# Layer normalization moved from GpSimd to VectorE, and query weights, bias copies and weight loads placed elsewhere

## The chip, the cores and the metric

The kernel runs on one core of a Trainium2 chip. A core has engines[...]: TensorE (PE in the profile, its weight loads PEld), VectorE (DVE), ScalarE (ACT), GpSimd (POOL) and SyncE (SP), which here only issues transfers. The metric is the device time of one execution in microseconds (us), lower is better.

## The reference

Inputs q, k and v are [8, 8, 576, 64] (batch, head, token, head dimension) in float32. The first part is a linear attention with positive features, the second a gated MLP with a mixing over tokens:

```python
def phi(x):
    proj = einsum('bhsd,df->bhsf', x, w_phi)              # 64 -> 128
    proj = proj - max(abs(proj), axis=-1, keepdims=True)
    return concatenate([exp(proj), exp(-proj)], axis=-1)
kv  = einsum('bhsf,bhsd->bhfd', phi(k), v)
z   = sum(phi(k), axis=2)
x   = einsum('bhsf,bhfd->bhsd', phi(q), kv) / (einsum('bhsf,bhf->bhs', phi(q), z)[..., None] + 1e-6)
h   = maximum(x_as_[8, 576, 512] @ w_in, 0)               # 512 -> 1024
u, v = h[..., :512], h[..., 512:]
v_n = (v - mean(v)) / sqrt(var(v) + 1e-6)                 # over the 512 features
v_s = einsum('ts,bsd->btd', w_spatial, v_n) + b_spatial[None, :, None]
out = (u * v_s) @ w_out
```

## The kernel before, in words

Each batch has 576 tokens: 512 main tokens, held as four groups of 128 on the partitions, and 64 tail tokens. Two batches form a group and share the partitions for their tails. The work is cut into 36 units: for each batch four units of two heads (main tokens), and for each group one tail unit. In order they are batch 0 (units 0, 1, 3, 4, with the tail of group 0 as unit 2 between them), batch 1 (5 to 8), the tail of group 1 (9), batch 2 (10 to 13), batch 3 (14 to 17), the tail of group 2 (18), batches 4 and 5 (19 to 26), the tail of group 3 (27), batches 6 and 7 (28 to 35).

The order of work is written out by a loop over steps, one for each unit. A step calls the stages in a fixed order: keys, queries, attention, sums, next, features, out, maxima. Each stage works on the unit that its lag gives, so that several units are in flight. After every stage `fill` takes tasks of the gated MLP from a queue by a credit of TensorE time, and so puts their matmuls between those of the attention. When a batch's attention is done, its tasks are queued: the v half (matmul, relu on ACT, statistics on DVE), the root, the normalization, the u half, the spatial product, and the output product. `at(i, f)` puts a load or a small job after step i. A helper, `pin`, keeps such instructions in program order; the profile gives all of them the line L61.

What the stages put on the engines:

- keys: `ps` (L267) on PE; the row maxima `mk` on DVE (L279); the exponentials `kf` on ACT (L282); the factors `em` on ACT (L302); on POOL the scaled values `vs` (L307), or for a tail `vst`, by `tail_scale`, two multiplications and a copy for each of two batches.
- queries: maxima `mq` on DVE (L293), their split into a high and a low part `mhl` (L296, L297), on DVE for the first five units and on POOL after. The maxima stage transposes `mhl` on PE (L328, `pt`).
- features: the projected queries minus their maxima, exponentiated as `qf` on ACT (L366). For units of batches 2 and up ("merged") one matmul does projection and subtraction (L345), with weights `wm`, which hold `wphi` for one of two heads and rows of minus one from `sel` for the maxima. Copies `qT_b` and `qt` on DVE (L331, L332) put the maxima beside the queries.
- sums and attention: `pv` from `vs` and `kf` (L379, L381) and `pn` from `kv` and `qf` (L399), the quotient `x` on DVE (L389, L390).
- the MLP: `pv` (L448), `vr` on ACT (L450), statistics on DVE (L451, L452), root on POOL (L458 to L461), normalization `vn` and for tails `vnt` on POOL (L465), `pu` (L503), the spatial product `ps` (L524, L525), the gate `uT` on DVE (L527), the output `po` (L549) and its copy `ob` (L552).

The spatial weights are loaded as `wsp`, `wspr` and `wspt` and transposed on PE (L216, L218, L225, L226) into `w_spT`, during the first batch's tasks. Its two bias rows are copied on ACT after that (L230, L233). PSUM is used as eight banks. Loads that convert to bf16 (k, q and the weights) are issued by POOL, the v loads and transposing loads by SP.

Of the kernel before, what the change touches and what calls it, by code (L numbers as in the profile page):

```python
# [8 lines left out]
FP32 = mybir.dt.float32  # L9
BF16 = mybir.dt.bfloat16  # L10
AF = mybir.ActivationFunctionType
ALU = mybir.AluOpType
# [4 lines left out]
def kernel(  # L17
# [15 lines left out]
    nc = tc.nc  # L33

    B, H, S, D = q.shape
    F = w_phi.shape[1]
    DM = moe_w_in.shape[0]
    DFF = moe_w_in.shape[1]
    HALF = DFF // 2
    P = 128  # L40
    KC = DM // P
    NP = H // 2
    NB = 4
    T0 = NB * P
    TL = S - T0
# [4 lines left out]
    cpool = ctx.enter_context(tc.tile_pool(name="const", bufs=1))  # L50
# [3 lines left out]
    small = ctx.enter_context(tc.tile_pool(name="small", bufs=3))  # L54
    s2 = ctx.enter_context(tc.tile_pool(name="stage_b", bufs=2))
# [4 lines left out]
    def pin(start):  # L60
        return lambda *a, **kw: tc.keep_in_program_order(start(*a, **kw))  # L61
# [12 lines left out]
    XB = 2  # L74
# [14 lines left out]
    def half_tile(x, b, y):  # L89
        if b not in st:  # L90
            alloc(b)
        if st[b][x][y] is None:
            n = f"{x}_bf{(2 * b + y) % 4}"
            st[b][x][y] = ld.tile([P, 4, NB * D], BF16, tag=n, name=n, bufs=1)
        return st[b][x][y]
# [44 lines left out]
    ident = cpool.tile([P, P], BF16)  # L140
# [3 lines left out]
    wphi2 = cpool.tile([P, 2 * F], BF16)  # L144
    pin(nc.vector.memset)(wphi2, 0.0)
    neghalf = cpool.tile([P, NB + 1], FP32)
    pin(nc.vector.memset)(neghalf, -0.5)

    w_spT = cpool.tile([P, NB + 2, S], BF16)
# [4 lines left out]
    for i in range(NM):  # L154
        for tiles, name in ((mhl, "mhl"), (mT, "mT")):
            t = cpool.tile([P, P], BF16, name=f"{name}{i}")
# [4 lines left out]
    wm = cpool.tile([P, H, F], BF16)  # L161
    sel1 = cpool.tile([P, H], BF16)
    sel = cpool.tile([P, H, F], BF16)
    pin(nc.vector.tensor_tensor)(out=sel1, in0=ident[:, 0:H], in1=ident[:, H:2 * H], op=ALU.add)
    pin(nc.vector.tensor_scalar)(out=sel, in0=sel1.unsqueeze(2).to_broadcast([P, H, F]), scalar1=-1.0,
                                 scalar2=None, op0=ALU.mult)
    vst = [cpool.tile([P, 2, 2, H, DA], BF16, name=f"vst{i}") for i in range(2)]
    vnt = [cpool.tile([P, 2, HALF], BF16, name=f"vnt{i}") for i in range(2)]
# [4 lines left out]
    def fill_vnt(i, copy):  # L173
        for bl, row in ((0, TL), (1, 0)):
            pin(copy)(out=vnt[i][:, bl, :], in_=ident[:, row:row + 1].to_broadcast([P, HALF]))

    pin(nc.scalar.copy)(out=vst[0].rearrange("p b s h d -> p (b s h d)"), in_=zero.to_broadcast([P, 4 * H * DA]))
    for y in range(2):
        r = slice(y * D, (y + 1) * D)
        pin(nc.scalar.copy)(out=wphi2[r, y * F:(y + 1) * F], in_=wphi_f[r, :])  # L180
    for i in range(2):
        fill_vnt(i, nc.gpsimd.tensor_copy)
    for x in ("k", "q"):
        pin(nc.gpsimd.tensor_copy)(out=half_tile(x, 0, 0)[:, 2:4], in_=first[x, 2])
    load("k", 0, 1, 0, 2)
# [5 lines left out]

    w_in_bf = cpool.tile([P, KC, DFF], BF16)
    w_out_bf = cpool.tile([P, KC, DM], BF16)
    wsp = s2.tile([P, NB, T0], BF16, tag="vn", name="wsp", bufs=2)
    wspr = cpool.tile([P, NB, TL], BF16)
    wspt = s2.tile([TL, S], BF16, tag="ob", name="wspt", bufs=6)
    bsp_row = s2.tile([P, S], FP32, tag="xT", name="bsp_row", bufs=3)
    nc.sync.dma_start(out=bsp_row[TL:TL + 1, :], in_=moe_b_spatial)
# [2 lines left out]
    rows = moe_w_spatial[0:T0, :].rearrange("(p c) s -> p c s", c=NB)  # L201
    cols = moe_w_in.rearrange("(kc p) f -> p kc f", p=P)
# [7 lines left out]
    def transpose_spatial(i):  # L210

        pt = psum.tile([P, S], BF16, tag="bank", name="pt")
        if i < NB:
            sc = POS[i]
            for tp, c in enumerate(POS):
                nc.tensor.transpose(out=pt[:, tp * P:(tp + 1) * P], in_=wsp[:, c, bass.ds(sc, P, step=NB)],  # L216
                                    identity=ident)
            nc.tensor.transpose(out=pt[:, T0:S], in_=wspt[:, bass.ds(sc, P, step=NB)],  # L218
                                identity=ident[:TL, :TL])
            nc.vector.tensor_copy(out=w_spT[:, i, :], in_=pt)  # L220
            return
        for bl in range(2):
            lo = bl * TL
            for tp, c in enumerate(POS):
                nc.tensor.transpose(out=pt[lo:lo + TL, tp * P:(tp + 1) * P], in_=wspr[:, c, :], identity=ident)  # L225
            nc.tensor.transpose(out=pt[lo:lo + TL, T0:S], in_=wspt[:, T0:S], identity=ident[:TL, :TL])  # L226
            nc.vector.tensor_copy(out=w_spT[lo:lo + TL, NB + bl, :], in_=pt[lo:lo + TL, :])
        for bl, row in ((0, TL), (1, 0)):
            r = slice(row, row + 1)
            pin(nc.scalar.copy)(  # L230
                out=w_spT[r, NB + bl, 0:T0].rearrange("o (a b p) -> o a b p", a=2, b=2),
                in_=bsp_row[r, 0:T0].rearrange("o (p b a) -> o a b p", a=2, b=2))
            pin(nc.scalar.copy)(out=w_spT[r, NB + bl, T0:S], in_=bsp_row[r, T0:S])  # L233


    def merged(u):
        return u["pair"] and u["b"] >= XB

    def weights_with_max(n):
        for j in range(4 * n, 4 * n + 4, 2):  # L240
            pin(nc.gpsimd.tensor_copy)(out=wm[:, j, :], in_=wphi2[:, 0:F])
            pin(nc.gpsimd.tensor_tensor)(out=wm[:, j + 1, :], in0=wphi2[:, F:2 * F], in1=sel[:, j + 1, :], op=ALU.add)
            pin(nc.gpsimd.tensor_copy)(out=wm[D:D + 2 * H, j, :], in_=sel[0:2 * H, j, :])

    def q_even(u):
        u["qE"] = qts[u["i"] % len(qts)]
# [205 lines left out]
        nc.vector.bn_aggr(out=mv[r], in_=stats[r])  # L452

    def root(mv, r, n):

        var = small.tile([P, NB, 1], FP32, tag="var", name="var")
        rs = small.tile([P, NB, 2], FP32, tag="rs", name="rs")
        nc.gpsimd.tensor_scalar(out=var[r, 0:n], in0=mv[r, 0:n, 1:2], scalar1=1e-6, scalar2=None, op0=ALU.add)  # L458
        nc.gpsimd.tensor_tensor(out=rs[r, 0:n, 0:1], in0=var[r, 0:n], in1=neghalf[r, 0:n].unsqueeze(2), op=ALU.pow)
        nc.gpsimd.tensor_tensor(out=var[r, 0:n], in0=mv[r, 0:n, 0:1], in1=rs[r, 0:n, 0:1], op=ALU.mult)  # L460
        nc.gpsimd.tensor_scalar(out=rs[r, 0:n, 1:2], in0=var[r, 0:n], scalar1=-1.0, scalar2=None, op0=ALU.mult)  # L461
        return rs

    def normalize(dst, src, rs):
        nc.gpsimd.tensor_scalar(out=dst, in0=src, scalar1=rs[:, 0:1], scalar2=rs[:, 1:2],  # L465
                                op0=ALU.mult, op1=ALU.add)

    def b_v(b, j):
        d = st[b]
# [8 lines left out]
    def b_root(b):  # L478
        st[b]["rs"] = root(st[b]["mv"], slice(0, P), NB)

    def b_ln(b, j):
        d = st[b]
        normalize(d["vn"][:, j, :], d["vr"][j], d["rs"][:, j, :])

    def b_v_tail(g, bls):
        d = gs[g]
        r = slice(bls[0] * TL, (bls[-1] + 1) * TL)
        vr = s2.tile([P, HALF], BF16, tag="vr", name="vr", bufs=5)
        stats = small.tile([P, 6], FP32, tag="stats", name="stats")
        mv = small.tile([P, 1, 2], FP32, tag="mv_t", name="mv_t")  # L490
        v_mm(lambda kc: d["xTt"][:, kc, r], vr, r, stats, mv[:, 0, :])
        rstd = root(mv, r, 1)
        for bl in bls:
            r = slice(bl * TL, (bl + 1) * TL)
            normalize(vnt[g % 2][r, bl, :], vr[r], rstd[r, 0, :])

    def b_u(b, dc):
        d = st[b]
# [176 lines left out]
    AT, AB, XP = 5, 6, 3  # L675
    io = {}

    def at(i, f, *a):
        io.setdefault(i, []).append(lambda: f(*a))

    at(1, load_v, 1)
    at(2, load, "k", 1, 0)
    at(2, load, "q", 1, 0)
    at(3, load, "k", 1, 1)
    at(3, load, "q", 1, 1)
    at(4, load_weight, w_in_bf[:, :, HALF:DFF], cols[:, :, HALF:DFF])
    at(4, load_weight, wspt, moe_w_spatial[T0:S, :])
    at(5, tail_scale, 0, 1)
    at(5, load_weight, wsp, rows[:, :, 0:T0])
    at(5, load_weight, wspr, rows[:, :, T0:S])  # L690
    at(6, load_weight, w_in_bf[:, :, 0:HALF], cols[:, :, 0:HALF])
    at(8, load_weight, w_out_bf, moe_w_out.rearrange("(kc p) f -> p kc f", p=P))
    for u in units:
        i = u["i"]
        if not u["pair"] and u["g"] > 0:
            early = 1 if u["g"] > 1 else 0
            at(i - AT - early, load_tail, "k", u["g"])
            for x in ("q", "v"):
                at(i - AT + 1 - early, load_tail, x, u["g"])
        if u["pair"] and u["b"] >= XB:  # L700
            if u["pj"] == 0:
                for n, (x, y) in enumerate((("k", 0), ("q", 0), ("k", 1), ("q", 1))):
                    at((4, 4, 6, 7)[n] if u["b"] == XB else i - AB + n, load, x, u["b"], y)
                for y in range(2):
                    at(i - AB + 1 + 2 * y, load_v, u["b"], y)
            for x in ("k", "q"):
                at(i - XP, cross, x, u)
    at(6, weights_with_max, 0)
    at(7, weights_with_max, 1)
    for u in units:  # L710
        if merged(u):
            at(u["i"] - 1, q_even, u)
# [36 lines left out]
```

## Time and profile before

| what | value |
|---|---|
| time, median of 3 runs | 283.42 us (283.27 to 283.42) |
| span of the profiled execution | 282.7 us |
| mean granted TensorE clock | 0.986 |
| busy: PE, DVE, ACT, POOL | 257.1, 231.2, 219.5, 200.5 us |
| POOL: vs L307 (64), vn L465 (32 of 128x512) | 65.5, 24.3 us |
| DVE: mk L279 (72), mq L293 (62) | 47.7, 39.8 us |
| DVE: statistics L451 (40), gate L527 (32) | 26.7, 22.0 us |
| shares of the chain that ended last: PE, POOL, ACT, DVE, DMA | 62, 12, 9, 6, 4% |

The busy time counts only the execution of instructions, not waiting. The chain that ended last is followed back from the last instruction, at each step to what released it; an engine with a large share of it held up the end, wherever its busy share is small. A wait for several semaphores is put down to the one that came last. Over 40 slices of the span (7.07 us each), the busy tenths of PE and POOL and the clock are:

```profile
PE   2777979986999999999999999999999999999993
POOL 5988999999859886799949974889548832511710
PEclk9979999999799999999999999999999999999999
```

### The profile page before, as it was taken

What the parts mean: (1) busy time and instruction counts of PE and PEld (TensorE: products, weight loads), DVE (VectorE), ACT (ScalarE), POOL (GpSimd) and SP (SyncE); (2) the same over time, 40 slices, a digit from 0 to 9 for tenths busy, and PEclk for the clock granted to TensorE, in tenths of its full rate; (3) what the DMA queues carried; (4) which work ended last, traced back from release to release, by engine and by line L of the source; (5) the groups of instructions that cost most, each with busy time, mean ns of one, the idle gap of its engine ahead of it and who ended that gap; (6) DMA issues with size and microseconds to landing.
All of it is one profiled execution on the core that took longest, in us unless ns stands there. A gap on an engine that the chain in (4) does not pass through costs nothing.

```text
span 282.7 us, 8134 instructions
## 1 busy us (share of the span) xinstructions
PE 257.1 (91%) x3001; PEld 173.1 (61%) x3042; DVE 231.2 (82%) x576; ACT 219.5 (78%) x499; POOL 200.5 (71%) x362
## 2 busy tenths in 40 slices
PE   2777979986999999999999999999999999999993
PEld 1466866754776667666666775766666765654441
DVE  7979987875799979998889989998889897566341
ACT  5689996978399997899889987899699977723601
POOL 5988999999859886799949974889548832511710
PEclk9979999999799999999999999999999999999999
DMA  7989999999986999989989999999766301120305
GB/s 205 238 205 125 152 144 217 111 164 195 225 87 163 130 243 196 162 206 210 214 96 130 207 252 138 200 214 217 86 122 132 86 2 68 46 77 37 112 3 186
DMA packets 85148, 42.43 MB, mean 150 GB/s; under 512 B 52146, under 2 KB 80498, under 8 KB 85108
## 3 DMA queue, kind: packets, MB, share of 16 engines
q1 hardware_dynamic: 60020, 30.95, 55.0%
q0 software_dynamic: 24928, 10.89, 34.9%
q8 instruction: 24, 0.39, 0.6%
q14 instruction: 16, 0.13, 0.2%
q10 hardware_dynamic: 160, 0.07, 0.1%
HBM read 32.85 MB, written 9.44 MB: 150 GB/s over the span
## 4 chain that ended last, share of the span: by engine, by line
PE 62%; POOL 12%; ACT 9%; DVE 6%; DMA 4%; issue 4%; SPq 0%; POOLq 0%; ACTq 0%; DVEq 0%
PE ps L524 9%; PE pv L448 9%; PE po L549 9%; PE ps L267 6%; PE pu L503 6%; ACT kf L282 5%; PE pv L379 4%; PE pn L399 4%; PE pq L345 3%; DMA q_bf<-in_q_dram 3%; PE ps L525 2%; POOL vs L307 2%; POOL vst L61 2%; DVE stats L451 2%; ACT qf L366 2%
## 5 line engine op out<-in xcount | busy, mean ns | idle before, releaser
L282 ACT ACTIVATE kf<-ps 128x512 bf16<-128x512 f32 x144 | 76.2, 637 | 9.9 <-DVE mk L279 9.5
L307 POOL TENSOR_TENSOR vs<-v_f,em 128x512 bf16<-128x512 f32 x64 | 65.5, 1044 | 19.0 <-ACT em L302 17.6
L366 ACT ACTIVATE qf<-pq 128x512 bf16<-128x512 f32 x128 | 66.6, 620 | 9.6 <-PE pq L345 8.5
L279 DVE TENSOR_REDUCE mk<-ps 128x4 f32<-128x512 f32 x72 | 47.7, 677 | 1.2 <-PE ps L267 0.5
L293 DVE TENSOR_REDUCE mq<-ps 128x4 f32<-128x512 f32 x62 | 39.8, 680 | 2.6 <-PE ps L267 1.4
L524 PE MATMUL ps<-w_spT,vn 128*128 128x512 bf16 x116 | 33.1, 384 | 3.6 <-POOL vn L465 3.1
L527 DVE TENSOR_TENSOR uT<-ps,uT 128x512 bf16<-128x512 f32 x32 | 22.0, 687 | 16.8 <-PE ps L525 16.8
L451 DVE BATCH_NORM_STATS2 stats<-vr 128x6 f32<-128x512 bf16 (+1 forms) x40 | 26.7, 684 | 7.3 <-ACT vr L450 6.9
L549 PE MATMUL po<-w_out_bf,uT 128*128 128x512 bf16 x121 | 32.0, 380 | 0.4
L503 PE MATMUL pu<-xT,w_in_bf 128*128 128x512 bf16 x121 | 31.5, 380 | 0.5 <-issue 0.2
L448 PE MATMUL pv<-w_in_bf,xT 128*128 128x512 bf16 x116 | 30.7, 380 | 0.7
L450 ACT ACTIVATE vr<-pv 128x512 bf16<-128x512 f32 (+1 forms) x40 | 23.5, 615 | 7.6 <-PE pv L448 5.9
L379 PE MATMUL pv<-vs,kf 128*128 128x66 bf16 x512 | 24.3, 194 | 1.3 <-ACT kf L282 1.3
L390 DVE TENSOR_TENSOR x<-pn,rc 128x256 bf16<-128x256 f32 x64 | 24.9, 417 | 0.3
L465 POOL TENSOR_SCALAR vn<-vr,rs 128x512 bf16<-128x512 bf16 x32 | 24.3, 766 | 1.1
L399 PEld LDWEIGHTS <-qf 128*128 128x128 bf16 x512 | 20.5, 99 | 7.1 <-issue 1.4
L505 ACT ACTIVATE uT<-pu 128x512 bf16<-128x512 f32 x32 | 19.7, 641 | 4.9 <-PE pu L503 3.2
L379 PEld LDWEIGHTS <-kf 128*128 128x128 bf16 x512 | 21.8, 97 | 2.5 <-issue 1.5
L552 ACT COPY ob<-po 128x512 f32<-128x512 f32 x18 | 11.0, 614 | 14.9 <-PE po L549 8.4
L399 PE MATMUL pn<-kv,qf 128*128 128x66 bf16 x512 | 22.0, 195 | 0.3 <-ACT qf L366 0.3
L381 PE MATMUL pv<-vst,kf 128*128 128x66 bf16 x128 | 21.2, 192 | 0.0
L524 PEld LDWEIGHTS <-vn 128*128 128x128 bf16 x128 | 11.7, 98 | 13.8 <-POOL vn L465 4.6
(133 smaller groups left out, 572.2 us busy)
## 6 DMA issues: line engine op xcount, KB each, us to landing
out_dram<-ob SPq DMA_DIRECT2D x32, 256.0 KB, 2.5
v_f<-in_v_dram SPq DMA_DIRECT2D x14, 512.0 KB, 7.0
k_bf<-in_k_dram POOLq DMA_DIRECT2D x14, 256.0 KB, 6.3
q_bf<-in_q_dram POOLq DMA_DIRECT2D x14, 256.0 KB, 6.4
qt<-qT_b SPq DMA_DIRECT2D x24, 64.0 KB, 4.2
v_tl<-in_v_dram SPq DMA_DIRECT2D x8, 128.0 KB, 3.4
v_f<-in_v_dram SPq DMA_DIRECT2D x1, 1024.0 KB, 9.4
w_in_bf<-in_moe_w_in_dram POOLq DMA_DIRECT2D x2, 512.0 KB, 10.5
```

The lines of the kernel that those rows point to most:

```text
L279: nc.vector.tensor_reduce(out=u["mk"][:, hs], in_=pk, axis=AX.X, op=ALU.max, apply_absolute_value=True)
L282: nc.scalar.activation(out=u["kf"][:, s, hs, :], in_=pk, func=AF.Exp, bias=0.0, scale=sc)
L293: nc.vector.tensor_reduce(out=mq[:, 4 * half:4 * half + 4], in_=pq, axis=AX.X, op=ALU.max, apply_absolute_value=True)
L307: nc.gpsimd.tensor_tensor(out=vs[:, s, :, 0:D], in0=st[u["b"]]["v"][:, pj * H:(pj + 1) * H, :], in1=em[:, s, :].unsqueeze(2).to_broadcast( ...
L366: nc.scalar.activation(out=qf[:, s], in_=pq, func=AF.Exp, bias=0.0, scale=sc)
L379: nc.tensor.matmul(out=pv[:, hh, s, :], lhsT=u["kf"][:, s, 4 * hh + c, :], rhs=u["vs"][:, s, 4 * hh + c, :], start=(c == 0), stop=False)
L399: nc.tensor.matmul(out=pn[:, pos, :], lhsT=u["qf"][hh][:, s, pos, :], rhs=d["kv"][:, 2 * u["pj"] + hh, s, :], start=(s == 0), stop=(s == 1))
L448: nc.tensor.matmul(out=pv[r], lhsT=lhs(kc), rhs=w_in_bf[:, kc, HALF:DFF], start=(kc == 0), stop=(kc == KC - 1))
L451: nc.vector.bn_stats(out=stats[r], in_=dst[r])
L503: nc.tensor.matmul(out=pu, lhsT=w_in_bf[:, kc, dc * P:(dc + 1) * P], rhs=d["xT"][:, kc, :], start=(kc == 0), stop=(kc == KC - 1))
L524: nc.tensor.matmul(out=ps, lhsT=d["vn"][:, sp, cs], rhs=w_spT[:, sp, 0:T0], start=(sp == 0), stop=False)
L549: nc.tensor.matmul(out=po[r], lhsT=lhs(dc), rhs=w_out_bf[:, dc, :], start=(dc == 0), stop=(dc == KC - 1))
```

## The change

It has four parts. The normalization of v moves from POOL to DVE: it takes (v - mean) * rs directly from the statistics, so the root needs two operations, one on DVE (variance plus epsilon) and the power on POOL, where before it had four on POOL. The merged query weights `wm` are built by three wide instructions at the start (two on ACT, one on POOL), where before twelve narrow ones on POOL came after steps 6 and 7. The bias copies of ACT come after steps 1 and 2 instead of behind the transposition of the spatial weights. The loads of the spatial weights become one transfer fewer (`wsp` takes all 576 columns, `wspr` goes) and, with those of w_in, w_out, the group-1 tail and batch 2, are placed at other steps. It is meant to unload POOL and to bring each load and copy when it is needed. Lines of the changed file stand up to four higher or lower than those above.

```diff
--- before.py
+++ after.py
@@ -180,6 +180,14 @@
         pin(nc.scalar.copy)(out=wphi2[r, y * F:(y + 1) * F], in_=wphi_f[r, :])
     for i in range(2):
         fill_vnt(i, nc.gpsimd.tensor_copy)
+    def alternate(t, i):
+        return t.rearrange("p (j two) f -> p j two f", two=2)[:, :, i, :]
+    pin(nc.scalar.copy)(out=alternate(wm, 0), in_=wphi2[:, 0:F].unsqueeze(1).to_broadcast([P, NP, F]))
+    pin(nc.scalar.copy)(out=alternate(wm[D:D + 2 * H], 0), in_=alternate(sel[0:2 * H], 0))
+    pin(nc.gpsimd.tensor_tensor)(out=alternate(wm, 1), in0=alternate(sel, 1),
+                                 in1=wphi2[:, F:2 * F].unsqueeze(1).to_broadcast([P, NP, F]), op=ALU.add)
     for x in ("k", "q"):
         pin(nc.gpsimd.tensor_copy)(out=half_tile(x, 0, 0)[:, 2:4], in_=first[x, 2])
     load("k", 0, 1, 0, 2)
@@ -191,8 +199,7 @@

     w_in_bf = cpool.tile([P, KC, DFF], BF16)
     w_out_bf = cpool.tile([P, KC, DM], BF16)
-    wsp = s2.tile([P, NB, T0], BF16, tag="vn", name="wsp", bufs=2)
-    wspr = cpool.tile([P, NB, TL], BF16)
+    wsp = s2.tile([P, NB, S], BF16, tag="vn", name="wsp", bufs=2)
     wspt = s2.tile([TL, S], BF16, tag="ob", name="wspt", bufs=6)
     bsp_row = s2.tile([P, S], FP32, tag="xT", name="bsp_row", bufs=3)
     nc.sync.dma_start(out=bsp_row[TL:TL + 1, :], in_=moe_b_spatial)
@@ -222,25 +229,21 @@
         for bl in range(2):
             lo = bl * TL
             for tp, c in enumerate(POS):
-                nc.tensor.transpose(out=pt[lo:lo + TL, tp * P:(tp + 1) * P], in_=wspr[:, c, :], identity=ident)
+                nc.tensor.transpose(out=pt[lo:lo + TL, tp * P:(tp + 1) * P], in_=wsp[:, c, T0:S], identity=ident)
             nc.tensor.transpose(out=pt[lo:lo + TL, T0:S], in_=wspt[:, T0:S], identity=ident[:TL, :TL])
             nc.vector.tensor_copy(out=w_spT[lo:lo + TL, NB + bl, :], in_=pt[lo:lo + TL, :])
-        for bl, row in ((0, TL), (1, 0)):
-            r = slice(row, row + 1)
-            pin(nc.scalar.copy)(
-                out=w_spT[r, NB + bl, 0:T0].rearrange("o (a b p) -> o a b p", a=2, b=2),
-                in_=bsp_row[r, 0:T0].rearrange("o (p b a) -> o a b p", a=2, b=2))
-            pin(nc.scalar.copy)(out=w_spT[r, NB + bl, T0:S], in_=bsp_row[r, T0:S])
+    def spatial_bias(bl):
+        r = slice(TL, TL + 1) if bl == 0 else slice(0, 1)
+        pin(nc.scalar.copy)(
+            out=w_spT[r, NB + bl, 0:T0].rearrange("o (a b p) -> o a b p", a=2, b=2),
+            in_=bsp_row[r, 0:T0].rearrange("o (p b a) -> o a b p", a=2, b=2))
+        pin(nc.scalar.copy)(out=w_spT[r, NB + bl, T0:S], in_=bsp_row[r, T0:S])

     def merged(u):
         return u["pair"] and u["b"] >= XB
-    def weights_with_max(n):
-        for j in range(4 * n, 4 * n + 4, 2):
-            pin(nc.gpsimd.tensor_copy)(out=wm[:, j, :], in_=wphi2[:, 0:F])
-            pin(nc.gpsimd.tensor_tensor)(out=wm[:, j + 1, :], in0=wphi2[:, F:2 * F], in1=sel[:, j + 1, :], op=ALU.add)
-            pin(nc.gpsimd.tensor_copy)(out=wm[D:D + 2 * H, j, :], in_=sel[0:2 * H, j, :])

     def q_even(u):
         u["qE"] = qts[u["i"] % len(qts)]
@@ -452,18 +455,14 @@
         nc.vector.bn_aggr(out=mv[r], in_=stats[r])

     def root(mv, r, n):
         var = small.tile([P, NB, 1], FP32, tag="var", name="var")
-        rs = small.tile([P, NB, 2], FP32, tag="rs", name="rs")
-        nc.gpsimd.tensor_scalar(out=var[r, 0:n], in0=mv[r, 0:n, 1:2], scalar1=1e-6, scalar2=None, op0=ALU.add)
-        nc.gpsimd.tensor_tensor(out=rs[r, 0:n, 0:1], in0=var[r, 0:n], in1=neghalf[r, 0:n].unsqueeze(2), op=ALU.pow)
-        nc.gpsimd.tensor_tensor(out=var[r, 0:n], in0=mv[r, 0:n, 0:1], in1=rs[r, 0:n, 0:1], op=ALU.mult)
-        nc.gpsimd.tensor_scalar(out=rs[r, 0:n, 1:2], in0=var[r, 0:n], scalar1=-1.0, scalar2=None, op0=ALU.mult)
+        rs = small.tile([P, NB, 1], FP32, tag="rs", name="rs")
+        nc.vector.tensor_scalar(out=var[r, 0:n], in0=mv[r, 0:n, 1:2], scalar1=1e-6, scalar2=None, op0=ALU.add)
+        nc.gpsimd.tensor_tensor(out=rs[r, 0:n], in0=var[r, 0:n], in1=neghalf[r, 0:n].unsqueeze(2), op=ALU.pow)
         return rs

-    def normalize(dst, src, rs):
-        nc.gpsimd.tensor_scalar(out=dst, in0=src, scalar1=rs[:, 0:1], scalar2=rs[:, 1:2],
-                                op0=ALU.mult, op1=ALU.add)
+    def normalize(dst, src, mv, rs):
+        nc.vector.tensor_scalar(out=dst, in0=src, scalar1=mv[:, 0:1], scalar2=rs, op0=ALU.subtract, op1=ALU.mult)

     def b_v(b, j):
         d = st[b]
@@ -480,7 +479,7 @@

     def b_ln(b, j):
         d = st[b]
-        normalize(d["vn"][:, j, :], d["vr"][j], d["rs"][:, j, :])
+        normalize(d["vn"][:, j, :], d["vr"][j], d["mv"][:, j, :], d["rs"][:, j, :])

     def b_v_tail(g, bls):
         d = gs[g]
@@ -492,7 +491,7 @@
         rstd = root(mv, r, 1)
         for bl in bls:
             r = slice(bl * TL, (bl + 1) * TL)
-            normalize(vnt[g % 2][r, bl, :], vr[r], rstd[r, 0, :])
+            normalize(vnt[g % 2][r, bl, :], vr[r], mv[r, 0, :], rstd[r, 0, :])

     def b_u(b, dc):
         d = st[b]
@@ -679,34 +678,41 @@
         io.setdefault(i, []).append(lambda: f(*a))

     at(1, load_v, 1)
+    at(1, spatial_bias, 0)
+    at(2, spatial_bias, 1)
     at(2, load, "k", 1, 0)
     at(2, load, "q", 1, 0)
     at(3, load, "k", 1, 1)
     at(3, load, "q", 1, 1)
     at(4, load_weight, w_in_bf[:, :, HALF:DFF], cols[:, :, HALF:DFF])
-    at(4, load_weight, wspt, moe_w_spatial[T0:S, :])
+    at(4, load, "k", 2, 0)
     at(5, tail_scale, 0, 1)
-    at(5, load_weight, wsp, rows[:, :, 0:T0])
-    at(5, load_weight, wspr, rows[:, :, T0:S])
-    at(6, load_weight, w_in_bf[:, :, 0:HALF], cols[:, :, 0:HALF])
-    at(8, load_weight, w_out_bf, moe_w_out.rearrange("(kc p) f -> p kc f", p=P))
+    at(5, load_weight, w_in_bf[:, :, 0:HALF], cols[:, :, 0:HALF])
+    at(5, load, "q", 2, 0)
+    at(6, load_tail, "k", 1)
+    at(6, load_weight, wspt, moe_w_spatial[T0:S, :])
+    at(7, load_tail, "v", 1)
+    at(7, load_tail, "q", 1)
+    at(7, load_weight, wsp, rows)
+    at(8, load, "k", 2, 1)
+    at(8, load_v, 2, 0)
+    at(9, load, "q", 2, 1)
+    at(9, load_v, 2, 1)
+    at(9, load_weight, w_out_bf, moe_w_out.rearrange("(kc p) f -> p kc f", p=P))
     for u in units:
         i = u["i"]
-        if not u["pair"] and u["g"] > 0:
-            early = 1 if u["g"] > 1 else 0
-            at(i - AT - early, load_tail, "k", u["g"])
+        if not u["pair"] and u["g"] > 1:
+            at(i - AT - 1, load_tail, "k", u["g"])
             for x in ("q", "v"):
-                at(i - AT + 1 - early, load_tail, x, u["g"])
+                at(i - AT, load_tail, x, u["g"])
         if u["pair"] and u["b"] >= XB:
-            if u["pj"] == 0:
+            if u["pj"] == 0 and u["b"] > XB:
                 for n, (x, y) in enumerate((("k", 0), ("q", 0), ("k", 1), ("q", 1))):
-                    at((4, 4, 6, 7)[n] if u["b"] == XB else i - AB + n, load, x, u["b"], y)
+                    at(i - AB + n, load, x, u["b"], y)
                 for y in range(2):
                     at(i - AB + 1 + 2 * y, load_v, u["b"], y)
             for x in ("k", "q"):
                 at(i - XP, cross, x, u)
-    at(6, weights_with_max, 0)
-    at(7, weights_with_max, 1)
     for u in units:
         if merged(u):
             at(u["i"] - 1, q_even, u)
```

## The prediction

> **What bounds the kernel now.** I read the share of busy time first, then the table of windows of 10 us, because the share is a mean over stages.
>
> ```profile
> PE 257.1 (91%) x3001; PEld 173.1 (61%) x3042; DVE 231.2 (82%) x576; ACT 219.5 (78%) x499; POOL 200.5 (71%) x362
> ```
>
> ```profile
> 40.00:50.00 10.00, 8.24 (x101) 5.78 (x100) 7.75 (x23) 7.65 (x19) 9.46 (x21) 1.00 1.64 200
> 60.00:70.00 10.00, 7.79 (x98) 5.37 (x97) 6.85 (x15) 8.80 (x22) 9.30 (x17) 1.00 1.30 187
> 70.00:80.00 10.00, 9.73 (x121) 7.05 (x123) 7.62 (x19) 4.74 (x11) 7.23 (x14) 0.83 1.36 209
> 110.00:120.00 10.00, 9.84 (x136) 6.89 (x136) 9.90 (x27) 8.80 (x22) 6.56 (x10) 1.00 1.18 164
> 150.00:160.00 10.00, 9.90 (x113) 6.57 (x112) 9.94 (x27) 9.57 (x24) 9.51 (x17) 1.00 1.14 181
> ```
>
> Columns: window, its length, then busy us (count) of PE, PEld, DVE, ACT, POOL; clock, DMA, GB/s. Two regimes show. From 40 to 70 us POOL is fullest and PE has holes. From 107 on PE has hardly any, and in the windows 110:120 and 150:160 DVE is as full as PE. Next, the chain that ended last, where POOL leads at two places:
>
> ```profile
> 64.47 1.06 POOL rs L459
> 67.90 2.28 POOL vn L465 x3
> 70.22 0.61 PE ps L524
> ...
> 264.56 1.05 POOL rs L459
> ...
> 267.07 2.27 POOL vn L465 x3
> 269.99 0.65 PE ps L524 x3
> ```
>
> The first is the end of a stretch of POOL work without a gap from 53.46 to 70.2. The second is the last normalization, with nothing else left to do. In the chain between about 104 and 205 there is only PE. Last, POOL's own timeline around unit 21, and ACT's:
>
> ```profile
> 116.84 2.04 POOL L61 TENSOR_TENSOR vst<-v_tl,em 64x512 bf16<-64x512 f32 x2 [1.95 <-ACT em L302]
> 119.14 2.04 POOL L61 TENSOR_TENSOR vst<-v_tl,em 64x512 bf16<-64x512 f32 x2
> 121.72 0.25 POOL L297 TENSOR_TENSOR mhl<-mq,mhl 128x8 bf16<-128x8 f32 x1
> 122.38 0.58 POOL L459 TENSOR_TENSOR rs<-var,neghalf 64x1 f32<-64x1 f32 x1
> ```
>
> ```profile
> 121.69 1.14 ACT L282 ACTIVATE kf<-ps 128x512 bf16<-128x512 f32 x2
> ```
>
> The tail's root stands on POOL behind two pairs of vst, although its statistics were ready at 118.5. Before the change only POOL waited for it.
>
> **What the Trainium skill says.** "VectorE: DVE Perf Modes", The perf-mode tier table and Side-by-side: a bf16 tensor_scalar within SBUF runs at four elements a cycle after about 150 cycles fixed, at 0.96 GHz; for 512 elements that is my estimate of 290 ns. The trace's nearest row agrees: the copy qt<-qT_b (L332, 16x512 bf16, 24 times) has a median of 285 ns. "SBUF — State Buffer", Who interferes with whom: DVE in such a mode and GpSimd exclude each other from one pair of ports for a whole instruction. L332 fits: its longest is 1564 ns and its mean 404 ns. "TensorE: Matmul & The Clock Gate", Part 1: a PE idle for too long gets half the clock; the trace has the clock at 0.5 from 70.2 to 73.6, after the wait for vn. "Perfetto Trace Analysis", Per-engine timelines: DVE, ACT and GpSimd take instructions strictly first in, first out. No trace can prove this, but it is what makes the new wait below dear.
>
> **The change part by part.**
>
> *POOL is relieved.* Away go 40 normalizations of 766 ns (30.6 us), three of the four operations of each of 16 roots (0.24 + 0.18 + 0.25 = 0.67, together 10.7 us), and twelve wm operations (4.0 us, all between 44.34 and 52.1). With about 1 us for the new wide operation POOL falls from 200.5 to about 156. In the steady part this is worth nothing directly: PE has no hole there that POOL causes.
>
> *DVE gets it.* 40 normalizations at 0.285 to 0.404 us, which is 11.4 to 16.2 us, and 16 variances at 0.17 (as bn_aggr) = 2.7 us; 14 to 19 in all, against 0.684 us each and 27 us if the fast mode were not entered. I take 0.36 us (most meet a busy POOL), so 17 us, or 2.1 per batch. The windows leave DVE about 0.9 us idle per 10 from 107 to 147, so about 1.8 per batch of 20 us. The sum fits barely, without room for waits.
>
> *DVE now waits for POOL's pow.* In the new order DVE does variance, one short operation, then the normalization, which must wait for the pow on POOL. Behind it in DVE's queue are the x of attention, qT_b, and the mk of the next unit, which kf on ACT needs, which the pv of attention on PE needs. By batch:
> - Batch 2's tail: DVE reaches vnt at 118.95; POOL can do the pow only after vst and mhl, with the variance gone from POOL at 122.06 to 122.64. DVE stands 3.7 us. In the trace of before the second mk ends at 121.6 and kf starts at 121.69, so kf has no slack there, and PE wants it at 123.5. PE loses about 3.
> - Batch 4's tail: the statistics are ready at 179.3, DVE reaches vnt near 180, POOL has vst to 181.5, mhl to 182.06, the q_bf issue to 183.16, the pow to 183.85. DVE stands 3 to 4 us, with two mk behind it. PE loses about 2.5.
> - The four-column roots (pow 1.05 us) and the tails of odd batches: 0.15 to 1.1 us each. PE's banks hold most of it; 0.5 for batch 1, 0.3 for 3, 0.5 for 5, nothing for 6 and 7, where DVE has room (11.2 of 20 in 240:260).
> Sum: 3 + 2.5 + 1.3 = +6.8.
>
> *Early stage.* Gains: PE's wait for POOL's mhl (1.5 us at 41.3, behind loads that now come later), the bias copies of ACT at 55.02 (2.5 us, of which PE waited 1.1 for qf), the waits for vn (2.4) and the half clock after them (about 1.6); 6.6 at the most. Losses: vnt and vn of batch 0 stand on DVE 2.5 us each, behind vs, vst and the k_bf issue on POOL; the second half of the q tail is issued at about 45 instead of before, lands 4.4 us later and is wanted at 48; wsp is issued at about 46 instead of 37.17, and PE wants it at 52.3. Before it took 7.7 us; w_out took 13.4 in that crowd (DMA 1.64 in 40:50). So each may cost nothing or 1 to 5 us. Net I take -1.5, with ends of -6 and +5.
>
> *Start.* The wide wm operations put 0.25 us of POOL before the casts of the first k and q, and the bias copies of 1.26 us each now fall after the em of unit 1 and at about 19.5, where ACT has 9.5 and DVE 10.0 of 10 busy just after: +0.75 (0.25 to 1.4).
>
> *End.* From 267.65 to 269.83 the first spatial product takes 2.18 us where its four matmuls need 1.07, since each waits for a vn of 0.77. DVE delivers one in 0.3: -1.1. The shorter root gives some 0.3 more and the hop between engines takes it back.
>
> Sum: +0.75 - 1.5 + 6.8 - 1.1 = +4.95; 283.4 + 4.95 = 288.4.
>
> **The rivals.**
> - *The relief of POOL wins (faster).* If ACT's em comes earlier, or PE's banks outlast the waits of DVE, the +6.8 shrinks to about +2, while early -6 and end -1.1 are had: 283.4 + 0.75 - 6 - 1.1 + 2 = 279. For it: POOL holds 12% of the chain, and the tails' vst run right behind the work that goes. Against it: kf's missing slack at 121.69.
> - *Everything cancels (same).* Early -5, DVE +5, start and end as above: 283.4 + 0.75 - 5 + 5 - 1.1 = 283.05. It needs an accident.
> - *Loads collide too (slower still).* If wsp comes 3.5 us late and the q tail 1.5, early turns from -1.5 to +3: 288.4 + 4.5 = 292.9. For it: the DMA share of 1.64 in 40:50. Against it: w_in is issued earlier, and wsp is one transfer instead of two.
>
> **How the numbers follow.** DVE's waits dominate, loads nearly on time: 0.40, 288.4. Loads collide too: 0.14, 292.9. Relief wins: 0.40, 279. Cancelling: 0.06. So slower 0.54, faster 0.40, same 0.06. The range from 277.0 to 293 reaches from the relief with a little more than its value to the collision.
>
> **What would show it.** Right: vnt of batches 2 and 4 on DVE preceded by an idle time of 3 us or more released by POOL rs; kf idle on mk just after, and holes in PE near 120 and 180; L465 near 0.3 to 0.4 us; the last ps group near 1.1 us. Wrong: L465 at 0.68 or more (then above 293); POOL's rs before DVE arrives at vnt, with windows of PE at 9.9 throughout (then below 280); PE waiting for wsp or q_tl near 50 would put the loss in the loads instead.

## The result, and the profile after

The changed kernel takes 301.95 us (median of 4 runs, 299.6 to 303.6), the kernel before 283.42 us (4 runs, 283.3 to 285.6); the ratio is 1.063 with a 95% interval of 1.054 to 1.072. It is slower, as forecast, but by 18.5 us where 5 were forecast, and outside the range. Here and below a median is of all executions of a kernel, while a ratio and its interval leave out the slow ones, in which the granted clock was lower. The page of the profiled execution (299.6 us, the shortest of the four; span 297.8 us), busy time of the engines and the chain that ended last:

```profile
PE 259.6 (87%) x3001; PEld 172.2 (58%) x3042; DVE 248.0 (83%) x632; ACT 221.8 (74%) x501; POOL 155.7 (52%) x262
PE 42%; DVE 18%; POOL 18%; DMA 6%; ACT 6%; issue 6%; SPq 2%; POOLq 0%; ACTq 0%; DVEq 0%
```

POOL has lost 44.8 us of work and DVE has gained 16.8, as reckoned (to about 156, and 17). Yet POOL's share of the chain went up from 12 to 18%, and DVE's from 6 to 18%. An engine with little work holds up more than before: that is what a wait looks like on a page of busy time. The windows (length, then busy us and count of PE, PEld, DVE, ACT, POOL) say when:

```profile
110.00:120.00 10.00, 9.84 (x143) 6.82 (x145) 9.81 (x25) 8.98 (x22) 5.67 (x9) 1.00 1.05 127
120.00:130.00 10.00, 7.31 (x75) 4.46 (x75) 6.50 (x17) 6.59 (x15) 5.26 (x10) 1.00 0.78 160
190.00:200.00 10.00, 6.38 (x70) 4.02 (x70) 7.07 (x20) 6.28 (x15) 4.62 (x9) 1.00 0.60 116
```

The last two windows in the kernel before:

```profile
120.00:130.00 10.00, 9.95 (x96) 6.08 (x95) 9.11 (x22) 9.39 (x22) 8.92 (x20) 1.00 0.89 192
190.00:200.00 10.00, 9.90 (x122) 6.90 (x121) 7.85 (x19) 8.57 (x22) 9.66 (x16) 1.00 1.31 207
```

In 120:130 and 190:200 of the changed kernel every engine is idle for between a quarter and a little over half of the time, so none is full there. They are not idle together: in under 1% of these windows do all four stand still at once. They wait for one another in turn. Just before the first of them, DVE was full. The waits of the whole execution (us in total, times, longest):

```profile
ACT kf L285 <- DVE mk L282: 18.6, 19, 3.7
DVE vnt L465 <- POOL rs L461: 11.1, 5, 4.0
DVE vn L465 <- POOL rs L461: 6.9, 8, 1.4
```

The second and third rows are new, 18.0 us of DVE idle. The first stood at half of that in the kernel before:

```profile
ACT kf L282 <- DVE mk L279: 9.5, 11, 2.1
```

DVE's timeline shows one of these waits, and ACT's what hung on it:

```profile
119.40 0.14 DVE L460 TENSOR_SCALAR var<-mv_t 64x1 f32<-64x1 f32 x1
119.47 0.41 DVE L393 TENSOR_TENSOR x<-pn,rc 128x256 bf16<-128x256 f32 x1
123.37 0.40 DVE L465 TENSOR_SCALAR vnt<-vr,mv_t,rs 64x512 bf16<-64x512 bf16 x1 [3.50 <-POOL rs L461]
125.70 0.65 DVE L282 TENSOR_REDUCE mk<-ps 128x4 f32<-128x512 f32 x1
126.70 0.69 DVE L282 TENSOR_REDUCE mk<-ps 128x4 f32<-128x512 f32 x1
```

```profile
126.38 2.12 ACT L285 ACTIVATE kf<-ps 128x512 bf16<-128x512 f32 x4 [3.21 <-DVE mk L282]
```

```profile
124.16 1.02 PE L451 MATMUL pv<-w_in_bf,xT 128*128 128x512 bf16 x4 [2.25 <-DVE x L393]
```

The last fence is PE's timeline. A normalization of 0.40 us waits 3.5 us; behind it stand an x that PE needs, whose own input rc was done at 119.4, and, after 2 us of other work, the mk of 125.70 that the first kf needs; ACT stops for 3.2 and PE for 2.25. Beside it POOL did just what was forecast:

```profile
120.03 2.04 POOL L61 TENSOR_TENSOR vst<-v_tl,em 64x512 bf16<-64x512 f32 x2
122.76 0.57 POOL L461 TENSOR_TENSOR rs<-var,neghalf 64x1 f32<-64x1 f32 x1
```

The variance was there at 119.5, and a power of 0.57 us came at 122.8, since POOL was at its vst and, after them, at three short instructions.

Since the order of PE's instructions did not change, the kernels can be laid side by side unit by unit. Here is the start of the first kf exponential of some units, and how much later it is than before (us, from the traces; the kernel without the power is explained below):

| kf of unit | before | changed | later by | no power, later by |
|---|---|---|---|---|
| 2 | 14.1 | 15.5 | 1.4 | 4.8 |
| 12 | 77.1 | 75.3 | -1.8 | 1.0 |
| 18 | 114.5 | 115.4 | 0.9 | 2.2 |
| 21 | 135.0 | 141.0 | 6.0 | 3.1 |
| 27 | 174.7 | 182.9 | 8.2 | 4.4 |
| 30 | 195.1 | 209.2 | 14.1 | 4.9 |
| 35 | 227.6 | 243.7 | 16.1 | 5.9 |
| end | 282.7 | 297.8 | 15.1 | 4.8 |

The early part gained 1.8 us and the end 1.0; all the loss, 17.9 us, is made between units 12 and 35, with two steps of 5 to 6 us at units 18 to 21 and 27 to 30. The ends of the table stand closer together than the medians do: the profiled execution of the kernel without the power (289.33 us) is the longest of its four, that of the changed kernel the shortest. So what a stretch costs is read from the table, and what a kernel costs from the medians.

### The profile page after: what moved, and what is told of

Same layout as the page of the kernel before. It is cut to its first block, busy times and chain, and to the rows that moved or that the text cites. A ratio compares the mean times of both kernels' runs of the same rounds, so it can differ in the third digit from the quotient of the medians.

```text
span 297.8 us, 8038 instructions
## 1 busy us (share of the span) xinstructions
PE 259.6 (87%) x3001; PEld 172.2 (58%) x3042; DVE 248.0 (83%) x632; ACT 221.8 (74%) x501; POOL 155.7 (52%) x262
## 4 chain that ended last, share of the span: by engine, by line
PE 42%; DVE 18%; POOL 18%; DMA 6%; ACT 6%; issue 6%; SPq 2%; POOLq 0%; ACTq 0%; DVEq 0%
PE ps L523 9%; POOL vs L310 6%; PE po L548 6%; PE pv L451 5%; DVE mq L296 5%; POOL vst L61 5%; DVE mk L282 5%; PE pu L502 4%; ACT kf L285 3%; PE ps L270 3%; POOL rs L461 3%; DMA out_dram<-ob 2%; SPq L61 2%; PE pv L382 2%; PE ps L524 2%
## 5 line engine op out<-in xcount | busy, mean ns | idle before, releaser
L461 POOL TENSOR_TENSOR rs<-var,neghalf 64x1 f32<-64x1 f32 (+1 forms) x16 | 12.7, 796 | 40.9 <-DVE var L460 29.5
L523 PE MATMUL ps<-w_spT,vn 128*128 128x512 bf16 x116 | 32.1, 379 | 0.6
L465 DVE TENSOR_SCALAR vn<-vr,mv,rs 128x512 bf16<-128x512 bf16 x32 | 16.1, 524 | 6.9 <-POOL rs L461 6.9
L61 POOL TENSOR_TENSOR vst<-v_tl,em 64x512 bf16<-64x512 f32 x16 | 16.4, 1038 | 10.4 <-ACT em L305 10.1
```

The costliest lines, as they stand in the source:

```text
L523: nc.tensor.matmul(out=ps, lhsT=d["vn"][:, sp, cs], rhs=w_spT[:, sp, 0:T0], start=(sp == 0), stop=False)
```

## The experiments

The theory: VectorE, which takes its instructions in order, now stops for a factor that GpSimd makes late, and everything behind it stops too. The rivals: the load of 40 normalizations on a VectorE that had no room; and the moved loads, copies and weight operations.

**One half of the change at a time.** The first kernel takes the normalization alone, the second the placement alone.

```diff
--- before
+++ e1_norm_alone
-        nc.gpsimd.tensor_scalar(out=var[r, 0:n], in0=mv[r, 0:n, 1:2], scalar1=1e-6, scalar2=None, op0=ALU.add)
+        nc.vector.tensor_scalar(out=var[r, 0:n], in0=mv[r, 0:n, 1:2], scalar1=1e-6, scalar2=None, op0=ALU.add)
...
-        nc.gpsimd.tensor_scalar(out=dst, in0=src, scalar1=rs[:, 0:1], scalar2=rs[:, 1:2], op0=ALU.mult, op1=ALU.add)
+        nc.vector.tensor_scalar(out=dst, in0=src, scalar1=mv[:, 0:1], scalar2=rs, op0=ALU.subtract, op1=ALU.mult)
--- changed
+++ e2_placement_alone
-        nc.vector.tensor_scalar(out=dst, in0=src, scalar1=mv[:, 0:1], scalar2=rs, op0=ALU.subtract, op1=ALU.mult)
+        nc.gpsimd.tensor_scalar(out=dst, in0=src, scalar1=rs[:, 0:1], scalar2=rs[:, 1:2], op0=ALU.mult, op1=ALU.add)
```

> The kernel before, with the root and the normalization as in the changed kernel and nothing else of the change. If the normalization on VectorE makes the loss (18.5 us in the comparison), this run shows nearly all of it: 299 to 304 us. If the moved loads, bias copies and wide weight operations make a good part of it, it stays below 292 us.

> The changed kernel with the root and the normalization back on GpSimd as before, so only the placement of weights, copies and loads is left of the change. If the normalization makes the loss: 280 to 284 us, perhaps a little faster than before, since unit 12 starts 1.8 us earlier in the changed kernel. If the placement makes the loss: over 290 us.

Measured: 306.17 us for the normalization alone (ratio 1.083, 1.077 to 1.089), 285.23 for the placement alone (1.005, 1.000 to 1.010). The normalization makes the loss, and more of it without the placement than with it: then the twelve narrow weight operations stand ahead of the first powers on POOL, and DVE's first wait is 4.9 us, where it is 2.8 in the changed kernel. From unit 12 to unit 35 the lag of the normalization alone grows from 4.8 to 22.7 us, so by 17.9 too (its clock is at half there for two stretches of 3.4 us, that of the changed kernel never), and that of the placement alone does not grow (1.3 and 1.2). The placement alone is worth nothing or a little less.

**Wait or load.** Two kernels separate them: one has the load and no wait, one the wait and hardly any load.

```diff
--- changed
+++ e3_no_pow
-        nc.vector.tensor_scalar(out=var[r, 0:n], in0=mv[r, 0:n, 1:2], scalar1=1e-6, scalar2=None, op0=ALU.add)
-        nc.gpsimd.tensor_tensor(out=rs[r, 0:n], in0=var[r, 0:n], in1=neghalf[r, 0:n].unsqueeze(2), op=ALU.pow)
+        nc.vector.tensor_scalar(out=rs[r, 0:n], in0=mv[r, 0:n, 1:2], scalar1=1e-6, scalar2=None, op0=ALU.add)
--- before
+++ e4_waits_alone
+    def wait_root(r, rs):
+        probe = small.tile([P, 2], FP32, tag="probe", name="probe")
+        nc.vector.tensor_copy(out=probe[r], in_=rs)
...
         normalize(d["vn"][:, j, :], d["vr"][j], d["rs"][:, j, :])
+        wait_root(slice(0, P), d["rs"][:, j, :])
```

> The changed kernel without the power: the variance plus epsilon itself is used as the factor, so GpSimd has no part in the normalization and VectorE waits for nothing new. The power is left out, so the outputs are of another scale. VectorE, TensorE and ScalarE have the same instructions in the same order. If VectorE's waits for the power on GpSimd (18.0 us of idle time in the changed kernel) make the loss: 282 to 288 us. If the load of 40 normalizations on VectorE makes it: 294 us or more.

> The kernel before, with normalization and root on GpSimd as they were, and in each place of a normalization one tiny VectorE copy (2 elements a partition) that waits for the finished root. This adds the wait for GpSimd and the order behind it, and almost no load. If the waits make the loss: 292 to 302 us. If the load makes it: 283 to 286 us.

Measured: 287.52 us without the power (1.017, 1.010 to 1.023), 311.57 with the waits alone (1.101, 1.096 to 1.107). With the same load, the same order of PE and ACT, and that of DVE but for two instructions, taking the wait away brings 14.4 us; in the table above the steps at units 18 to 21 and 27 to 30 fall from 5.1 and 5.9 us to 0.9 and 0.5. ACT's wait falls too. The tiny copies cost more than the whole change: the root they wait for still has four operations on POOL, the normalizations stand there too, and DVE's waits are nearly twice as long. The row of the first kernel and that of the second are:

```profile
ACT kf L285 <- DVE mk L282: 6.0, 10, 1.5
DVE probe L470 <- POOL rs L461: 32.6, 16, 6.5
```

Leaving out the power also takes 12.3 us of work off POOL. The next two kernels leave that work in place.

**The wait mended without changing the work.** Only the tail's normalization, then all of them, are put later in DVE's order; `pin` keeps them where they are put.

```diff
--- changed
+++ e5_tail_later
-        rstd = root(mv, r, 1)
+        d["tail"] = vr, mv, root(mv, r, 1)
+
+    def b_ln_tail(g, bls):
+        vr, mv, rstd = gs[g]["tail"]
         for bl in bls:
...
             ts += ns[y:y + 1] + outs[2 + y:3 + y] + us[y:y + 1]
+            if y == 1:
+                ts.append((0.0, lambda: b_ln_tail(g, [bl])))
...
-        nc.vector.tensor_scalar(out=dst, in0=src, scalar1=mv[:, 0:1], scalar2=rs, op0=ALU.subtract, op1=ALU.mult)
+        pin(nc.vector.tensor_scalar)(out=dst, in0=src, scalar1=mv[:, 0:1], scalar2=rs, op0=ALU.subtract, op1=ALU.mult)
--- e5_tail_later
+++ e6_all_later
-            ts += ns[y:y + 1] + outs[2 + y:3 + y] + us[y:y + 1]
+            ts += outs[2 + y:3 + y] + us[y:y + 1] + ns[y:y + 1]
```

> The changed kernel, with the tail's normalization issued by a task of its own between the main normalizations and kept there in VectorE's order, so that the power is long done when VectorE gets to it. Load, power and TensorE order stay. If VectorE's place in the queue makes the loss: the 11.1 us of waits before vnt go, 6.9 us before vn stay, 288 to 293 us. If the load makes it, or any use of a factor from GpSimd: 298 us or more.

> As the run with the later tail, and each main normalization one place later too, behind the output and u tasks that followed it. If waits make the loss: nearly what the kernel without the power took, 285 to 290 us, and VectorE idle before L465 below 4 us. If the load makes it: 298 us or more.

Measured: 291.95 us (1.028, 1.022 to 1.035) and 289.93 us (1.020, 1.014 to 1.026). Moving eight instructions back in a queue gives 10 of the 18.5 us, and the other 32 give 2 more. In the second kernel DVE's wait for the factor is, of 18.0 us:

```profile
DVE vn L61 <- POOL rs L461: 2.7, 3, 1.2
```

Four kernels have the same work on DVE and differ in these waits; in the two with later normalizations some 16 to 18 other DVE instructions stand at another place than in the changed kernel too. From unit 12 to unit 35, where the clock is full in all four traces (us):

| kernel | DVE's waits for the factor | growth of the lag | above the first row |
|---|---|---|---|
| no power | 0 | 4.9 | |
| all later | 1.1 | 6.5 | 1.6 |
| tail later | 3.8 | 8.9 | 4.0 |
| changed | 12.4 | 17.9 | 13.0 |

Each microsecond that DVE waits for the factor costs about a microsecond of time.

**What is left: load and relief.** The kernel without waits and the one with hardly any stay 4 to 6 us above the kernel before. One kernel adds the load to the kernel before without taking anything off POOL, one adds it twice; a third relieves POOL and adds no load.

```diff
--- before
+++ e9_load_alone
+    def more_load(r, src, mv):
+        for i in range(1):
+            t = s2.tile([P, HALF], BF16, tag="load", name="load", bufs=2)
+            nc.vector.tensor_scalar(out=t[r], in0=src, scalar1=mv[:, 0:1], scalar2=mv[:, 1:2], op0=ALU.subtract, op1=ALU.mult)
--- e9_load_alone
+++ e10_load_twice
-        for i in range(1):
+        for i in range(2):
--- changed
+++ e11_no_norm
-        d["vr"][j] = s2.tile([P, HALF], BF16, tag="vr", name="vr", bufs=5)
+        d["vr"][j] = d["vn"][:, j, :]
...
-        normalize(d["vn"][:, j, :], d["vr"][j], d["mv"][:, j, :], d["rs"][:, j, :])
```

> The kernel before, whose GpSimd still does root and normalization, with one more VectorE instruction beside each of the 40: the same tensor_scalar with the same tiles, with mean and variance as factors, into a tile that nothing reads. It waits for nothing of GpSimd. If the load of VectorE makes what is left in the kernels without waits (about 4.9 us from unit 12 to unit 35 in the kernel without the power): 286 to 290 us beside a before of 284. If VectorE had room: 283.5 to 285 us.

> As the run with one more instruction, with two (80 in all). If VectorE is full in the steady part, the second set costs at least as much as the first, as it finds less room: 292 to 302 us. If VectorE had room: below 287 us.

> The changed kernel without root and normalization: relu writes v straight into the tiles of the spatial product, statistics are still taken. So GpSimd is relieved and VectorE carries nothing more; the normalization is left out, and the outputs are of another scale. TensorE's order is the same. If relieving GpSimd alone is worth nothing where TensorE has no holes: 282 to 286 us, and the kernel without the power stands some 3 to 5 us above it, which is then the price of VectorE's load. If the relief is worth as much as the load costs (the extra instructions with a busy GpSimd cost 14.7 us, with a relieved one about 4): 276 to 280 us.

Measured: 299.3 us (1.051, 1.046 to 1.056) for the load, 309.0 us (1.081, 1.074 to 1.088) for twice the load, 282.55 us (0.992, 0.989 to 0.994) for the relief. The load alone missed its expectation by 9 us at least: it costs 14.7 us, as much as the waits. Twice the load missed it too, and the second set of instructions costs 8 us by the ratios' executions and 10 by the medians, less than the first, where at least as much was expected. The relief alone gives 2.3 us, as the expectation for worthless relief had it; the lag of its kf changes by 0.3 us from unit 12 to 35, so in the steady part the relief of POOL by itself is worth nothing. (Its profile has a span of 284.1 us, longer than its median time, so only this difference is read from it.) So the two halves depend on each other: 40 instructions on DVE cost 12.3 us from unit 12 to unit 35 beside a busy POOL (0.9 to 13.2 later), and 4.9 us beside a relieved one (1.0 to 5.9, in the kernel without the power). One place in the timeline of the load alone shows how, first DVE, then POOL, then PE:

```profile
164.96 0.67 DVE L279 TENSOR_REDUCE mk<-ps 128x4 f32<-128x512 f32 x1
165.66 2.76 DVE L332 COPY qt<-qT_b 16x512 bf16<-16x512 bf16 x1
168.45 0.69 DVE L279 TENSOR_REDUCE mk<-ps 128x4 f32<-128x512 f32 x1
```

```profile
164.74 1.51 POOL L465 TENSOR_SCALAR vn<-vr,rs 128x512 bf16<-128x512 bf16 x2
166.23 2.04 POOL L307 TENSOR_TENSOR vs<-v_f,em 128x512 bf16<-128x512 f32 x2
168.23 0.26 POOL L309 CAST vs<-em 128x32 bf16<-128x32 f32 x1
```

```profile
170.44 0.60 PE L427 MATMUL pn<-kv,qf_t 128*64 128x66 bf16 x8 [3.08 <-DVE mq L293]
```

A copy whose median is 285 ns took 2.76 us: it began during the second of four instructions (two vn, two vs) that POOL ran without a gap, and ended 0.15 us after the last of them, with an mk behind it. This fits what the Trainium skill says in "SBUF — State Buffer", Who interferes with whom, of the ports that DVE in a fast mode and GpSimd share: the instruction that comes first keeps them for its whole length, and the other engine is blocked. Here the engine that came second waited not for one instruction but for a run of them. PE then stood for 3.08 us, and its clock is at half from 170.3 to 173.7 us, which is in the 12.3 us too (1.7 us at most, an estimate from half speed for 3.4 us); the trace without the power has no such stretch there. Summed over the qt copies of the merged units and the added instructions, the time above the median of each is 10.7 us in the kernel with the load alone. In the kernel without the power it is 2.8 us for these copies and the normalizations together. The difference, 7.9 us, is near the 7.4 us by which the load costs more there. That these ports are the whole reason is an inference from this agreement and is not shown: DVE's order was not the same in the two kernels. Of the 575 DVE instructions that all these kernels have in common, some 20 stand at another place in DVE's order in the changed kernel and in the one without the power than in the kernel before, and some 14 in the one with the load alone. So 4.9 us is the price of the load and of that order together, and no run has the one without the other.

**The start and the end.** Two kernels take the end's gain without the rest, and one of them also puts the bias copies back; the last one mends the start of the kernel with all normalizations later.

```diff
--- before
+++ e7_last_batch
-        normalize(d["vn"][:, j, :], d["vr"][j], d["rs"][:, j, :])
+        normalize(d["vn"][:, j, :], d["vr"][j], d["rs"][:, j, :], nc.vector if b == B - 1 else nc.gpsimd)
--- e2_placement_alone
+++ e8_placed_no_bias
-        normalize(d["vn"][:, j, :], d["vr"][j], d["rs"][:, j, :])
+        normalize(d["vn"][:, j, :], d["vr"][j], d["rs"][:, j, :], nc.vector if b == B - 1 else nc.gpsimd)
...
-    at(1, spatial_bias, 0)
-    at(2, spatial_bias, 1)
--- e6_all_later
+++ e12_mended
-    at(1, spatial_bias, 0)
-    at(2, spatial_bias, 1)
```

In the last two, `transpose_spatial` calls `spatial_bias` for both rows at its end, where the copies were before.

> The kernel before, with the four main normalizations of the last batch alone on VectorE and all else on GpSimd. At the end nothing stands behind VectorE, and each spatial product waits for less: 1.1 us off the stretch from the last root to the end, 282.0 to 282.9 us beside a before of about 283.5. If the waits for GpSimd there are hidden: no change.

> The kernel before with the changed kernel's wide weights and load places, but bias copies back behind the spatial transposition, and the last batch's four main normalizations on VectorE. If the bias copies ahead of kf make the loss of the start, the exponentials of unit 2 start at 14.1 us as before and not at 15.5 to 15.8, and the time is 281 to 283 us. If the wide weights make it, unit 2 stays late, and the time is 283 us or more.

> The kernel with all normalizations later, with the bias copies back behind the spatial transposition. If ScalarE's wait for the bias row (3.4 us in that kernel, with kf behind it) makes the loss of the start: unit 2's exponentials start at 14.1 us instead of 17.9, and the time falls by about 3 us to 286 to 288 us. If the wide weight operations make it: no fall, 289 to 291 us.

Measured: 283.67 us beside 284.12 (0.998, 0.996 to 1.001), 284.02 (0.999, 0.996 to 1.002), and 290.08 us (1.017, 1.009 to 1.025). In the traces the end does shorten: with the last batch on DVE the lag goes from 0.3 at unit 35 to -0.8 at the end, so 1.1 us. But that is too little to stand clear of the spread of the times, and neither kernel is shown to be faster than the one before. With the bias copies back, the kf of unit 2 starts at 14.1 us in both kernels that have it. In the others the trace shows what held it; this is ACT in the kernel with all normalizations later:

```profile
16.64 1.24 ACT L61 CAST w_spT<-bsp_row 1x512 bf16<-1x512 f32 x2 [3.40 <-DMA bsp_row<-in_moe_b_spatial_dram]
17.89 2.06 ACT L285 ACTIVATE kf<-ps 128x512 bf16<-128x512 f32 x4
```

The copy was ready to be issued, but not its row of bias, a small transfer queued on SP behind the v loads. So ACT, in order, waits, for 1.3 to 4.7 us in the traces, for data that are not read for another 50 us (in this kernel the first product with these rows starts at 71.1). Yet no gain shows in the time: 290.08 against 289.93 us, where the expectation had 286 to 288; one of the four executions took 286.6, the others 290.1 to 290.5. By unit 12 the kernels with a late start had caught up (-0.5 with the wait, -1.2 without), and the mended one lost 3.5 us at units 25 to 26, where the other lost 2.0. PE stands for 1.66 us at that place in both, but only the mended one's clock is at half afterwards, from 165.5 to 168.9 us. That costs 1.7 us at most (an estimate from half speed for 3.4 us), about the difference of 1.5; why the clock fell in one and not in the other is open.

## Why the prediction was wrong in size

Point by point, by the prediction's own steps:

- *What bounds the kernel, and the direction*: right. DVE's waits came where they were named and as long as forecast: 3.5 us before vnt of batch 2 (3.7 forecast) and, in the trace, 3.96 for batch 4 (3 to 4 forecast), each followed by a wait of kf for mk and holes in PE.
- *The waits' price*: this is the step that failed. The sum had +6.8 for all waits of the steady part: 3 for batch 2, 2.5 for batch 4 and 1.3 for the small ones, mostly held by PE's banks. Against the kernel without the power the waits cost 13.0 us from unit 12 to unit 35: batch 2's step 4.2 us (5.1 less 0.9), batch 4's 5.4 (5.9 less 0.5), the rest 3.4. By the medians all waits together cost 14.4. The waits themselves were forecast well, 12.4 us in this stretch; what failed is the part of each that was to be absorbed. The two long waits cost more than they lasted, and the small ones, 5.0 us in all, are mostly not held by the banks. That nothing is caught up because DVE has too little room is argued from its windows, not tested by itself.
- *Two readings of the trace of before*: the mk that ends at 121.6 is the first of its unit, not the second, which ends at 122.6; the first kf waits for the first, so the missing slack stands. And the chain from 104 to 205 has one step that is not PE's, 0.69 us of DVE at 172.2.
- *The load*: "The sum fits barely, without room for waits" was written, and then nothing was charged for it. Without any wait the load, with the order of DVE that came with it, costs 4.9 us between units 12 and 35. Its size was near (16.8 us against 17): the normalizations have a median of 0.41 us, so the estimate of 290 ns was too low, and a mean of 0.52 for vn, since a few take over 1.1 us.
- *The relief of POOL in the steady part*: worth nothing by itself, as said, but beside it DVE's load costs 4.9 and not 12.3 us, which was not seen.
- *The early part and the start*: forecast -1.5 and +0.75, together -0.75; measured -1.8 at unit 12. It is a sum: the lag is 2.3 us at unit 11, and then 4.1 are gained by unit 12, where the forecast had 2.4 for the waits for vn and 1.6 for the half clock after them; the changed kernel's clock stays full. The feared collision of the loads did not come, though in the start the bias copies found a wait that the forecast had not: it priced the copies, and not the row that they copy.
- *The end*: forecast -1.1, measured -1.0 (16.1 to 15.1). The last products of the profile after show no wait for vn; four of them take 1.08 us each, as those of before took from the second on:

```profile
284.06 0.86 PE ps L523 x4
285.14 0.65 PE ps L523 x3
286.22 0.86 PE ps L523 x4
287.30 0.86 PE ps L523 x4
```

In place of +0.75 - 1.5 + 6.8 - 1.1 = +4.95, the profiled run, whose span is 15.1 us longer, reads: -1.8 up to unit 12, +4.9 of load (from the kernel without the power), +13.0 of waits (17.9 - 4.9), -1.0 at the end.

## What to carry to other kernels

Before moving an instruction to a faster engine, look where its operands come from: if one comes late from a third engine, the move turns that engine's idle wait into a stop of a full queue, and here the same 40 instructions put later in the queue brought back 12 of 18.5 us. On an engine as full as DVE here, charge a wait in full: its 12.4 us of waits cost 13.0. Added work was cheaper, 15.8 us of it costing 4.9 beside a relieved GpSimd, but not free. And price a copy moved earlier by the arrival of what it copies, not only by its own length.

## What the runs showed that was not expected

The cost of 40 VectorE instructions of the same kind was 4.9 us with a relieved GpSimd and 12.3 us with a busy one, and a copy of 285 ns stretched to 2.76 us beside a run of GpSimd instructions. A wait of 3.4 us at the start of the kernel left no clear trace in the time, since by unit 12 both kernels stood within 0.7 us of each other. And the same idle time of 1.66 us on PE was followed by half clock in one kernel and by full clock in the other.
